# The same instructions in another order: 860 words of a hand-ordered list for attention and an MLP

## The chip, the cores and the metric

The kernel runs on one core of a Trainium2 chip. The metric is the device time of one execution in microseconds; runs are compared by the median of several. The engines are TensorE (PE, with its weight loads as PEld), VectorE (DVE), ScalarE (ACT), GpSimd (POOL) and SyncE (SP), which only issues DMAs. Each engine works through its own instructions strictly in the order in which the program gives them, and waits for other engines by semaphores.

## The reference

Attention with a causal mask and a bias from a running sum, over 8 batches of 8 heads, 576 rows and 64 columns, then a layer norm and a two-layer MLP (512 to 2048 to 512) with a residual:

```python
scores = scale * np.matmul(q, k.transpose(0, 1, 3, 2))
cum = np.cumsum(np.maximum(s, 0.0), axis=-1)
bias = -(cum[:, :, :, None] - cum[:, :, None, :])
scores = np.where(causal, -1000000000.0, scores + np.minimum(bias, 0.0))
attn = np.exp(scores - np.max(scores, axis=-1, keepdims=True))
attn = attn / (np.sum(attn, axis=-1, keepdims=True) + 1e-09)
x = np.matmul(attn, v)            # heads side by side: (8, 576, 512)
xn = (x - mu) / np.sqrt(var + 1e-06) * g_ln
out = x + np.maximum(xn @ w_ch1, 0.0) @ w_ch2
```

## The kernel before

Rows are taken in tiles of 128 (four, and a tail of 64 rows, tile 4). The work of a batch is: load k, q and v; transpose k and q; scores in PSUM banks; exp on ScalarE into the SBUF tile `er`; a mask on the diagonal blocks on GpSimd; the product with v; a division by the row sums on VectorE; the layer norm's statistics and the normalised rows `xn`; a transpose of those by DMA; the first product with w1 and relu (into `hT`); the second product with w2; scale, residual and store.

All of it is one straight program. A fixed opening issues the first loads, mostly on GpSimd's queue, which also converts them. After it the order is a list of 1238 words, `PLAN` (L1278), written out by hand: a word such as `vm.2.0:P` names a step, its arguments and, behind a colon, the engine (A ScalarE, D VectorE, P GpSimd). A loop calls the steps one after another, and each step issues its few instructions on its engines. The list thus sets the order on each engine, and only that: two words that are neighbours in the list but on different engines have no order between them beyond what data and buffers ask.

The words that matter here:

- The running sums of the bias, in three pieces of bf16: `relu`, `relur` and `scan.0/1/2` (the scan over columns 0 to 127, 128 to 255, 256 to 575), `hi`, `sub`, `mid`, `lo` split a piece, `tc` transposes the pieces on PE and `bc` copies them into the rows of k and q (L281, L285). `m` is two memsets (L1219).
- Batch 0, tile by tile: `cq`, `ck` convert the first tile of q and k (L140); `T.t.g` transposes tile t of head group g on PE (L948, into a bank `trt`), `e.t.g` copies it out to `kq`; `S.t.g.i` is a bank of scores, `x` its exp (L987); `V` the product with v (L1028), `N` its division, `L.t` the normalised rows, `X.t` their transposes on PE, `y.t` the copy out; `M` and `r` are a first product in pieces and its relu.
- Batch 1, head by head: `Q.k.n`/`Q.q.n` transposes a pair of heads (L322, `trqk`), `E...0` and `E...1` copy its halves out; `aug` and `a3` bring the bias rows by DMA on SP (L264, L266); `s` scores and exp, `d` the tail, `v` product, `n` division, `l` the normalised rows, `D` their transpose by DMA on SP (L732).
- Batches 2 to 7, by pairs of heads: `lr.b.t` loads tile t of k and q on SP, `cr.b.t.u` converts it on GpSimd (L217), `tr` transposes by DMA on SP (L224); `lv.b.t` loads v on SP (L205), `vm.b.t` weighs it on GpSimd (L232). Batch 2 has its k and q from GpSimd's own loads (`lp`) with `O2`, `F` and `G` (copy, transposes, copy out; L360). `B2.n` is a burst of six banks of scores for pair n (L548), `bx.n.x` one exp of the six (L553), `bm.n.x` one mask (L492), `sd`, `se`, `sm` the same for the tail keys; `Y.n.i` is the product with v for head i of the pair (L627), `K.n.i` its division; `ga` and `la` make statistics and normalised rows, `Da` their transpose by DMA.
- `u` and `U` each run one unit of the MLP from a queue: four matmuls of 512 columns, of the first product with a relu behind it (on ScalarE for `u`, on VectorE for `U`; L761, L750, L752) or of the second (L780), after whose last quarter VectorE makes the result (L792) and SP stores it (L813).
- `w2.n` loads a quarter of w2 on GpSimd's queue. `to` closes the first set of PSUM banks (2 for `trt`, `ph` and `py`, 3 for scores, 2 for transposes and products, 1 more) and opens the second (2 for products and `py`, 6 for bursts and `ph`).

Buffers are slots: 8 for loaded rows of 128 x 512 f32, 6 more for v from `to` on, `er` for four heads. A step that needs a slot waits until the last user of an earlier tenant is done, wherever in the list that user stands on its own engine.

Of the kernel before, what the change touches and what calls it, by code (L numbers as in the profile page):

```python
# [16 lines left out]
P = 128  # L17
# [13 lines left out]
def fast_path(  # L31
# [13 lines left out]
    B, H, S, D = q.shape  # L45
# [13 lines left out]
    G = 4  # L59
# [881 lines left out]
    E = {"A": "act", "D": "dve", "P": "pool"}  # L941
# [241 lines left out]
    def raise_flag(count, ones, n):  # L1183
# [95 lines left out]
        relur.1 lr.3.0 relu.0 scan.0 scan.1 cq hi.0 qu.1 hi.1 sub.0 mid.0 lo.0 relur.2 sub.1 scan.2 W.2  # L1279
        tc.0 bc.0 ck.0 T.0.1 T.0.0 mid.1 lo.1 tc.1 e.0.1:D bc.1 T.1.1 hi.2 sub.2 e.0.0:A S.0.0.0 T.1.0  # L1280
        W.1 m mid.2 lo.2 La.3 tc.2 e.1.1:D x.0.0.0 V.0.0 bc.2 e.1.0:A S.0.1.0 N.0.0 x.0.1.0 S.1.1.0
        x.1.1.0 T.2.1 bc.4 e.2.1:D S.1.1.1 x.1.1.1 T.2.0 S.1.0.1 x.1.0.1 e.2.0:D V.0.1 S.1.0.0 N.0.1
        S.2.1.2 x.2.1.2 T.3.0 x.1.0.0 e.3.0:D qu.2 S.2.0.2 S.2.1.0 x.2.0.2 aug L.0 x.2.1.0 T.3.1 S.3.0.1
        x.3.0.1 V.1.0 e.3.1:D qu.3 La.2 N.1.0 V.1.1 N.1.1 L.1 S.2.0.0 x.2.0.0 S.2.0.1 x.2.0.1 S.3.0.2
        x.3.0.2 X.0 y.0:A S.3.1.2 S.2.1.1 x.2.1.1 V.2.0 N.2.0 x.3.1.2 X.1 y.1:D S.3.0.0 x.3.0.0 V.2.1
        M.0.1.0 B.0.1 M.0.1.3 S.3.0.3 x.3.0.3 M.0.1.2 N.2.1 L.2 M.0.1.1 r.0.1:A M.0.0.0 M.0.0.2 Q.q.4
        B.1.1 O E.q.4.0:A M.0.0.3 E.q.4.1:A V.3.0 N.3.0 S.3.1.1 x.3.1.1 M.0.0.1 r.0.0:D S.3.1.3 S.3.1.0
        T.4.0 e.4.0:D X.2 y.2:D x.3.1.3 Q.k.4 E.k.4.0:D T.4.1 e.4.1:D x.3.1.0 S.4.0.1 x.4.0.1 S.4.0.0
        M.0.2.0 M.0.2.2 x.4.0.0 M.0.2.3 V.3.1 E.k.4.1:D N.3.1 B.2.1 S.4.1.1 x.4.1.1 u d.8 L.3 M.0.2.1
        Q.q.5 r.0.2:D B.1.0 s.8 u X.3 S.4.1.0 x.4.1.0 y.3:D Sk xk E.q.5.1:D E.q.5.0:A B.0.0 B.3.0 a3 u  # L1290
        v.8 qu.4 qu.5 Q.k.5 lp.9 E.k.5.0:D u E.k.5.1:D V.4.0 N.4.0 s.9 cr.3.0.1 n.8 V.4.1 N.4.1 Q.q.6
        E.q.6.0:A u B.2.0 d.10 s.10 wr Q.k.6 E.k.6.0:D A.0 v.9 lp.10 w2.2 lr.3.1 E.k.6.1:D n.9 u U
        E.q.6.1:A s.11 Q.k.7 Q.q.7 E.q.7.0:A lp.11 La.6 E.k.7.0:D E.q.7.1:A U U E.k.7.1:D v.10 n.10
        cr.3.0.0 U d.12 s.12 U v.11 n.11 ga.1.0.0 A.2 d.14 s.13 O2.k.9:A u w2.3 B.3.1 v.12 n.12 ga.1.0.3
        s.14 O2.k.8:A A.1 me wT lv.2.0 wx vo.2:P U v.13 n.13 ga.1.1.2 s.15 cr.3.1.1 U O2.q.9:A ga.1.0.2
        F.k.8 v.14 ga.1.0.1 F.k.9 G.k.9:A n.14 U u A.3 R vm.2.0:P lr.3.2 v.15 cr.3.2.0 O2.k.11:A lv.2.1
        lv.2.2 vm.2.1:P G.k.8:A ga.1.1.1 u lv.2.3 u O2.q.8:A ga.1.1.3 F.q.9 G.q.9:A n.15 ga.1.2.1
        O2.q.11:A lv.2.4 lr.3.3 cr.3.2.1 cr.3.1.0 ga.1.2.0 ga.1.1.0 ga.1.2.3 ga.1.2.2 l.0 O2.k.10:A u u
# [4 lines left out]
        K.8.0 bx.9.5 K.8.1 bm.9.3 bx.9.2 bm.9.0 bx.9.3 bx.9.1 bm.9.1 u bm.9.2 U u u Y.9.0 vm.3.0:P  # L1303
        ga.1.2.4 la.1.4 B2.10 bx.10.0 K.9.0 bx.10.3 bx.10.4 bx.10.2 bx.10.5 cr.3.4.0 bm.10.3 bx.10.1
        Y.9.1 U K.9.1 u u tr.3.2.4 U u tr.3.4.5 bm.10.1 Y.10.1 lv.3.1 bm.10.0 B2.11 bx.11.0 bx.11.4
        lv.3.2 bx.11.5 lv.3.3 K.10.1 bm.10.2 Y.10.0 K.10.0 bm.11.2 ga.2.0.0 lv.3.4 bx.11.2 bm.11.0 La.4
        bx.11.1 u ga.2.1.2 ga.2.0.3 U u tk.3 cr.4.1.1 lr.4.2 bx.11.3 Y.11.0 K.11.0 bm.11.3 u sd.3 U
        bm.11.1 u se.3 ga.2.0.1 lr.4.3 cr.4.0.1 vm.3.1:P Y.11.1 K.11.1 lv.4.0 lv.4.1 vm.3.4:P lr.4.4 u
# [273 lines left out]
```

## Time and profile before

| | |
|---|---|
| runs shown | 348.24 us median of 3 (347.27 to 348.98) |
| the profiled execution | 347.05 us around a span of 345.5 us |
| mean granted TensorE clock | 0.992 |
| instructions | 8016, of them 3067 matmuls |
| HBM | 37.11 MB read, 9.44 MB written |

The profile is of one execution. A span is the time from the first to the last instruction. In its lines, `out<-in` are the program's tiles, xN counts instructions, and what stands in brackets or behind an arrow is the idle time of the engine just ahead of an instruction and what ended it. Views used below: the page (shares of the engines, and 40 slices of the span in tenths), windows (busy time of each engine in stretches), waits (who waited for whom), groups of instructions by line and shape, the timeline of an engine (start, length, what), and the chain of waits that ended last.

### The profile page before, as it was taken

Reading aid. Unit: us, or ns where it says so; the run is one execution under the profiler, and the core shown is the slowest. Engines: PE = TensorE matmul, PEld = TensorE weight load, DVE = VectorE, ACT = ScalarE, POOL = GpSimd, SP = SyncE. Lnnn points to the kernel's source line nnn. Section 1 sums busy time; section 2 is a strip of 40 time slices with the busy share of each in tenths; the row PEclk is TensorE's granted clock in tenths of the full one; section 3 lists DMA queues with packets and bytes.
Section 4 is the critical chain, followed back from the end, with each engine's and each line's share of the span. In section 5 each row is a group of like instructions: output and inputs, shape, how many; then the busy total and the mean of one; then the engine's idle time right before and its main releaser. Section 6 shows DMA issues by size and latency. Waiting matters only on the chain.

```text
span 345.5 us, 8016 instructions
## 1 busy us (share of the span) xinstructions
PE 332.2 (96%) x3067; PEld 185.6 (54%) x3093; DVE 206.6 (60%) x593; ACT 185.4 (54%) x343; POOL 168.8 (49%) x306
## 2 busy tenths in 40 slices
PE   5999999989999999999999999999999999999994
PEld 2998856545545555555555555554545444444443
DVE  6687798826675687556653774557448614523412
ACT  4698889677655686357636863486434204202200
POOL 8897677696577775865685377441301001000000
PEclk9899999999999999999999999999999999999998
DMA  9999999899989999998686965600420141011022
GB/s 147 185 191 174 201 194 204 191 221 237 202 197 241 224 223 196 225 216 183 154 190 176 227 112 138 139 2 2 113 71 0 23 132 46 2 76 47 0 64 65
DMA packets 147963, 48.59 MB, mean 141 GB/s; under 512 B 135281, under 2 KB 143761, under 8 KB 147921
## 3 DMA queue, kind: packets, MB, share of 16 engines
q1 hardware_dynamic: 121856, 38.34, 51.2%
q0 software_dynamic: 24304, 8.92, 21.6%
q10 hardware_dynamic: 1760, 0.79, 0.9%
q8 instruction: 25, 0.41, 0.5%
q14 instruction: 18, 0.14, 0.1%
HBM read 37.11 MB, written 9.44 MB: 135 GB/s over the span
## 4 chain that ended last, share of the span: by engine, by line
PE 82%; SPq 6%; DMA 4%; POOL 3%; DVE 2%; issue 1%; ACT 0%
PE ph L761 32%; PE py L780 32%; PE pot L627 7%; SPq L205 5%; DMA rowtmp<-in_v_dram 3%; PE sa L548 2%; PE trt L948 2%; PE sc L548 1%; PE sb L548 1%; DMA c_in<-in_s_dram 1%; POOL v_bf L232 1%; PE ph L1072 1%; PE st L970 1%; POOL kq L217 1%; PE pot L1028 1%
## 5 line engine op out<-in xcount | busy, mean ns | idle before, releaser
L780 PE MATMUL py<-w_bf,hT 128*128 128x512 bf16 (+2 forms) x583 | 128.4, 367 | 1.8 <-issue 0.3
L761 PE MATMUL ph<-xT,w_bf 128*128 128x512 bf16 x480 | 109.8, 379 | 0.0
L752 ACT ACTIVATE hT<-ph 128x512 bf16<-128x512 f32 x97 | 58.0, 602 | 82.0 <-PE ph L761 80.6
L780 PEld LDWEIGHTS <-hT 128*128 128x128 bf16 x608 | 56.1, 98 | 60.9 <-issue 0.7
L761 PEld LDWEIGHTS <-w_bf 128*128 128x128 bf16 x544 | 51.0, 98 | 56.3
L492 POOL TENSOR_SCALAR_AFFINE_SELECT er<-er 128x256 bf16<-128x256 bf16 x96 | 38.5, 415 | 61.8 <-ACT er L553 46.9
L792 DVE SCALAR_TENSOR_TENSOR yo<-py,rstd,xb 128x512 f32<-128x512 f32 x32 | 24.0, 751 | 48.5 <-PE py L780 44.2
L750 DVE TENSOR_SCALAR hT<-ph 128x512 bf16<-128x512 f32 x39 | 26.8, 690 | 27.0 <-PE ph L761 26.2
L553 ACT ACTIVATE er<-sb 128x512 bf16<-128x512 f32 x48 | 28.2, 609 | 21.1 <-PE sb L548 21.1
L553 ACT ACTIVATE er<-sa 128x512 bf16<-128x512 f32 x48 | 28.6, 608 | 13.3 <-PE sa L548 10.5
L232 POOL TENSOR_TENSOR v_bf<-rowtmp,wt 128x512 bf16<-128x512 f32 (+1 forms) x30 | 32.4, 1085 | 1.9 <-DMA rowtmp<-in_v_dram 1.8
L627 PEld LDWEIGHTS <-er 128*128 128x128 bf16 x672 | 25.7, 97 | 10.8 <-POOL er L492 1.5
L553 ACT ACTIVATE er<-sc 128x512 bf16<-128x512 f32 x48 | 28.8, 613 | 4.1 <-PE sc L548 4.1
L627 PE MATMUL pot<-v_bf,er 128*128 128x66 bf16 x672 | 28.1, 193 | 1.1 <-POOL er L492 1.0
L684 POOL TENSOR_TENSOR rstd<-rstd,mhalf 128x4 f32<-128x4 f32 (+1 forms) x8 | 8.8, 1097 | 38.8 <-DVE rstd L683 35.7
L644 DVE TENSOR_REDUCE sums<-pot 128x5 f32<-128x10 f32 x48 | 8.0, 166 | 31.2 <-PE pot L627 30.9
L710 DVE SCALAR_TENSOR_TENSOR xn<-xb,mv,gb 128x512 bf16<-128x512 f32 x28 | 25.2, 898 | 1.0
L217 POOL CAST kq<-rowtmp 128x512 bf16<-128x512 f32 (+1 forms) x30 | 20.7, 699 | 8.9 <-DMA rowtmp<-in_k_dram 8.8
L669 DVE BATCH_NORM_STATS2 stats<-xb 128x6 f32<-128x128 f32 (+1 forms) x84 | 23.8, 323 | 0.4
L647 DVE TENSOR_TENSOR xb<-pot,rinvs 128x256 f32<-128x256 f32 x48 | 20.4, 425 | 1.6
L548 PEld LDWEIGHTS <-kq 64*128 64x128 bf16 x360 | 11.2, 94 | 10.1 <-issue 4.7
L987 ACT ACTIVATE er<-st 128x512 bf16<-128x512 f32 x24 | 13.1, 604 | 3.6 <-PE st L978 2.3
(172 smaller groups left out, 394.9 us busy)
## 6 DMA issues: line engine op xcount, KB each, us to landing
out_dram<-yo SPq DMA_DIRECT2D x32, 256.0 KB
rowtmp<-in_v_dram SPq DMA_DIRECT2D x24, 256.0 KB
rowtmp<-in_k_dram SPq DMA_DIRECT2D x20, 256.0 KB
rowtmp<-in_q_dram SPq DMA_DIRECT2D x20, 256.0 KB
w_bf<-in_moe_w_ch_dram POOLq DMA_DIRECT2D x8, 512.0 KB, 9.3
kp<-in_k_dram POOLq DMA_DIRECT2D x8, 144.0 KB, 9.4
qp<-in_q_dram POOLq DMA_DIRECT2D x8, 144.0 KB, 9.8
v_bf<-in_v_dram POOLq DMA_DIRECT2D x8, 128.0 KB, 7.7
```

Source lines behind the costliest of these rows:

```text
L217: nc.gpsimd.tensor_copy(out=rows[b % 2][0:pn, t, u], in_=loaded.pop(("kq"[u], b, t))[0:pn])
L232: e.tensor_tensor(out=v_bf[b % 2][0:pn, t, :, 0:D], in0=loaded.pop(("v", b, t))[0:pn], in1=wt[0:pn, t, b, :].unsqueeze(2).to_broadcast([pn ...
L492: nc.gpsimd.affine_select(out=out, in_=out, compare_op=ALU.is_ge, fill=0.0, base=0, pattern=pattern, channel_multiplier=-1,)
L548: nc.tensor.matmul(a, lhsT=lhsT, rhs=rhs, start=True, stop=True)
L553: nc.scalar.activation(out=er[:, 2 * n % 4 + i, o : o + 512], in_=bank["B", n].pop((name, i)), func=ACT.Exp, scale=scale,)
L627: nc.tensor.matmul(pot[:, t, :], lhsT=cols, rhs=v_bf[b % 2][:, kb, h, :], start=(kb == 0), stop=(kb == t),)
L710: nc.vector.scalar_tensor_tensor(out=xn, in0=tiles[t], scalar=mvs[b][:, t, 0:1] if b > 0 else mean0[:, t : t + 1], in1=gb, op0=ALU.subtrac ...
L750: nc.vector.tensor_scalar_max(out=dst, in0=ph, scalar1=0.0)
L752: nc.scalar.activation(out=dst, in_=ph, func=ACT.Relu)
L761: nc.tensor.matmul(ph, lhsT=w1_bf[:, kd, fb * P : (fb + 1) * P], rhs=xT[:, :, kd, :], start=(kd == 0), stop=(kd == KD - 1),)
L780: nc.tensor.matmul(py[t], lhsT=hT[:, fb, t * P : (t + 1) * P], rhs=w2_bf[:, fb, c0:c1], start=(fb == 0), stop=(fb == FB - 1),)
L792: nc.vector.scalar_tensor_tensor(out=yo, in0=py[t], scalar=rs, in1=x[:, c0:c1], op0=ALU.mult, op1=ALU.add)
```

## The change

The list's first 860 words stand in another order; each word occurs as often as before, and the remaining 378 are the same. Seventeen copies and evictions change engines: to VectorE go `e.1.0`, `y.0`, `r.0.1`, `E.q.4.1`, `E.q.5.0`, `E.q.6.0`, `E.q.7.0`, `E.q.7.1`, `G.k.8` and `G.k.11`; to ScalarE `e.2.1`, `e.4.0`, `E.k.4.0`, `r.0.2`, `E.k.5.0`, `E.k.6.1` and `E.k.7.0`. There are 112 `u` and 19 `U` among the 860 words before and after, at other places. In the diff, cut to the stretches that the text speaks of, the lines of the list are as they stand:

```diff
     PLAN = """
-        relur.1 lr.3.0 relu.0 scan.0 scan.1 cq hi.0 qu.1 hi.1 sub.0 mid.0 lo.0 relur.2 sub.1 scan.2 W.2
-        tc.0 bc.0 ck.0 T.0.1 T.0.0 mid.1 lo.1 tc.1 e.0.1:D bc.1 T.1.1 hi.2 sub.2 e.0.0:A S.0.0.0 T.1.0
...
-        T.4.0 e.4.0:D X.2 y.2:D x.3.1.3 Q.k.4 E.k.4.0:D T.4.1 e.4.1:D x.3.1.0 S.4.0.1 x.4.0.1 S.4.0.0
...
-        lr.3.4 vm.2.3:P vm.2.2:P cr.3.3.0 u F.q.8 G.q.8:A F.q.11 G.q.11:A u u O2.q.10:A F.k.10 G.k.10:A
-        F.k.11 G.k.11:A tk.2 qu.6 qu.7 l.1 l.2 l.3 u D F.q.10 G.q.10:A cr.3.3.1 vm.2.4:P to u lv.3.0
-        B2.8 bx.8.3 bx.8.0 vo.3:P bx.8.2 ga.1.0.4 u lr.4.0 lr.4.1 u ga.1.1.4 bx.8.4 bm.8.2 sd.2 se.2
-        sm.2 bx.8.5 bx.8.1 bm.8.0 bm.8.3 bm.8.1 cr.3.4.1 u tr.3.0.2 u B2.9 Y.8.0 bx.9.0 bx.9.4 Y.8.1
...
+        m relu.0 relur.1 scan.0 scan.1 hi.0 hi.1 W.2 sub.0 sub.1 mid.1 cq mid.0 W.1 lo.1 ck.0 lo.0 tc.0 bc.0
+        tc.1 T.0.1 e.0.1:D T.0.0 relur.2 bc.1 S.0.1.0 T.1.1 T.1.0 scan.2 e.0.0:A e.1.1:D hi.2 x.0.1.0 O S.0.0.0
...
+        x.1.0.0 T.3.1 L.0 N.1.1 e.2.1:A S.2.0.0 V.1.0 N.1.0 S.3.0.2 x.2.0.2 x.2.0.0 X.0 L.1 S.2.1.1 x.2.0.1
+        x.2.1.1 S.2.1.2 V.2.0 S.3.0.0 X.1 S.3.0.3 x.2.1.2 y.0:D x.3.0.0 S.2.1.0 x.2.1.0 e.3.1:D M.0.0.0 M.0.0.2
...
+        E.q.4.0:A x.3.1.3 M.0.1.3 S.3.1.2 M.0.0.3 S.3.1.0 L.2 x.3.1.2 X.2 Q.k.4 S.3.1.1 T.4.0 x.3.0.1 r.0.1:D
+        e.4.0:A La.3 qu.3 r.0.0:D x.3.1.0 T.4.1 V.3.0 y.2:D qu.4 M.0.2.0 x.3.1.1 S.4.0.1 E.k.4.0:A u x.4.0.1
...
+        E.q.6.1:A u a3 E.k.6.0:D V.4.1 E.q.6.0:D n.9 qu.5 lv.2.2 s.10 u N.4.1 d.10 U s.11 Q.k.7 O2.k.8:A v.10
...
+        O2.q.10:A l.3 ga.1.0.1 cr.3.3.0 F.q.10 u O2.q.11:A u O2.k.11:A l.1 l.2 D U F.q.11 F.k.11 lv.2.0 u lv.2.1
+        G.k.11:D G.k.10:A tk.2 lr.3.2 lr.3.4 u to G.q.10:A vm.2.4:P lv.3.2 B2.8 cr.3.0.0 G.q.11:A cr.3.1.0
+        bx.8.0 u ga.1.2.4 bx.8.5 bx.8.3 sd.2 bm.8.3 U bx.8.4 u vo.2:P bx.8.1 bx.8.2 B2.9 u bm.8.2 bm.8.0 se.2
+        bx.9.4 bx.9.1 bx.9.0 qu.6 vm.2.0:P bm.8.1 u u bx.9.2 u vm.2.1:P bx.9.5 sm.2 cr.3.2.0 U bm.9.3 cr.3.4.0
+        bx.9.3 u cr.3.2.1 lv.3.0 Y.8.0 B2.10 bm.9.0 cr.3.4.1 bm.9.2 K.8.0 tr.3.0.2 bx.10.0 tr.3.4.5 Y.8.1
...
```

More of the change, by code (lines that the diff above doesn't have):

```diff
@@ L1289, in fast_path @@
[L1289 to L1298, printed above, removed]
@@ L1304, in fast_path @@
[L1304 to L1308, printed above, removed]
@@ L1359, in fast_path @@
-        u u u vl u u u u u u u u u u u u u u u u u u
+        m relu.0 relur.1 scan.0 scan.1 hi.0 hi.1 W.2 sub.0 sub.1 mid.1 cq mid.0 W.1 lo.1 ck.0 lo.0 tc.0 bc.0
+        tc.1 T.0.1 e.0.1:D T.0.0 relur.2 bc.1 S.0.1.0 T.1.1 T.1.0 scan.2 e.0.0:A e.1.1:D hi.2 x.0.1.0 O S.0.0.0
+        sub.2 mid.2 lo.2 V.0.1 x.0.0.0 e.1.0:D S.1.1.0 x.1.1.0 tc.2 bc.2 qu.1 V.0.0 bc.4 aug S.1.0.1 T.2.0
+        x.1.0.1 S.1.1.1 La.4 T.3.0 S.1.0.0 N.0.1 x.1.1.1 e.2.0:D T.2.1 N.0.0 V.1.1 S.2.0.2 e.3.0:D qu.2 S.2.0.1
+        x.1.0.0 T.3.1 L.0 N.1.1 e.2.1:A S.2.0.0 V.1.0 N.1.0 S.3.0.2 x.2.0.2 x.2.0.0 X.0 L.1 S.2.1.1 x.2.0.1
@@ new lines, in fast_path @@
+        bm.30.3 bx.31.1 bm.31.1 Y.30.1 K.30.1 ga.7.1.0 ga.7.0.4 bm.31.3 ga.7.1.4 ga.7.1.3 bx.31.4 bm.31.2 u U
+        Y.31.1 U bm.31.0 ga.7.1.2 u Y.31.0 K.31.0 K.31.1 ga.7.2.2 ga.7.2.3 ga.7.2.0 u u ga.7.1.1 ga.7.2.4 u u u
+        U ga.7.0.0 u u u u ga.7.2.1 la.7.0 la.7.1 la.7.2 la.7.3 Da.7.0 u u u u u u u u u u u u u u u u u U u U u
+        la.7.4 U u U u u u u U U gd u Da.7.4 u u u u u u u u u u u u u u u u U u u u U U U u u U u U U U U fl u
+        u u u u u vl u u u u u u u u u u u u u u u u u u
```

114 lines of the change are left out of this document (56 added, 58 removed).

## The prediction

> **What bounds the kernel now.** I read the page first, for the shares of the engines.
>
> ```profile
> span 345.5 us, 8016 instructions
> ...
> PE 332.2 (96%) x3067; PEld 185.6 (54%) x3093; DVE 206.6 (60%) x593; ACT 185.4 (54%) x343; POOL 168.8 (49%) x306
> ...
> PEclk9899999999999999999999999999999999999998
> DMA  9999999899989999998686965600420141011022
> ```
>
> PE is busy for 332.2 of 345.5 us, so only the 13.3 us without a matmul, and whatever runs at a lower clock, can be won by an order. DMA is full for the first third. The windows say where the idle time lies (first number the length, second PE busy; then weight loads, DVE, ACT, POOL, the clock, the DMA share and GB/s).
>
> ```profile
> 5.40:8.80 3.40, 1.30 (x11) 0.64 (x10) 2.57 (x10) 1.93 (x5) 3.33 (x7) 1.00 1.64 184
> 8.80:12.20 3.40, 3.11 (x33) 2.90 (x30) 2.24 (x7) 1.38 (x2) 2.72 (x4) 0.50 2.14 163
> ...
> 15.60:32.00 16.40, 15.41 (x322) 14.91 (x320) 14.12 (x43) 13.69 (x26) 14.74 (x25) 1.00 1.62 186
> 32.00:56.00 24.00, 23.53 (x344) 16.91 (x341) 20.19 (x49) 20.75 (x41) 17.08 (x33) 1.00 1.33 194
> 56.00:70.00 14.00, 13.58 (x126) 7.67 (x127) 10.82 (x31) 11.10 (x19) 10.51 (x18) 1.00 1.00 202
> 70.00:77.00 7.00, 5.94 (x60) 2.96 (x59) 2.03 (x4) 5.49 (x11) 6.71 (x16) 1.00 1.00 223
> 77.00:175.00 98.00, 97.39 (x945) 52.23 (x951) 65.55 (x197) 61.14 (x117) 66.80 (x124) 1.00 0.98 206
> ```
>
> Length less PE busy is 0.99, 0.47, 0.42 and 1.06 us in the four stretches from 15.6 to 77, and 0.61 in the 98 us behind them. From 77 us on there is next to nothing to win; the changed words reach to about 247 us, so there the new order can only hold what is. The last view names the waits of PE.
>
> ```profile
> PE trt L948 <- DVE rowb L285: 1.6, 1, 1.6
> PE idle L858 <- DVE warm L875: 1.5, 1, 1.5
> PE pot L627 <- POOL er L492: 1.0, 1, 1.0
> PE trqk L322 <- DVE xT L142: 0.6, 1, 0.6
> PE after L1369 <- DVE mark L1367: 0.5, 1, 0.5
> ...
> PE trt L948 <- DVE rowb L281: 0.3, 1, 0.3
> PE trx L743 <- DVE xn L710: 0.3, 1, 0.3
> PE py L780 <- DMA w_bf<-in_moe_w_ch_dram: 0.3, 1, 0.3
> ```
>
> The rows shown add up to 6.1 us. The first memset (1.5) and the end mark (0.5) stay; with three small rows left out, some 5 us are the most that a better order can take away, apart from the half-clock stretch.
>
> **The change, part by part.** No instruction is added or removed and none changes shape, so PE's own work stays. Each term below is a wait that moves.
>
> *The start.* These rows show what T.0.1 (the first L948) is late for.
>
> ```profile
> 3.48 0.34 DVE L925 CAST identf<-ident 64x64 f32<-64x64 bf16 x1
> 4.20 0.28 DVE L1196 SCALAR_TENSOR_TENSOR hT<-hT 64x128 f32<-64x128 f32 x1 [0.38 <-DMA hT<-in_s_dram]
> ...
> 6.58 0.28 DVE L311 TENSOR_TENSOR hT<-c_sc,c 64x128 f32<-64x128 f32 x1
> ...
> 7.29 0.60 ACT L140 CAST rowb<-tiletmp 128x512 bf16<-128x512 f32 x1
> 7.42 0.88 DVE L292 TENSOR_TENSOR_SCAN c_sc<-c_one,c_sc,c_in 64x320 f32<-64x320 f32 x1 [0.57 <-ACT c_in L1222]
> 8.53 1.64 PE L948 MATMUL trt<-ident,rowb 128*68 128x128 bf16 x16 [1.61 <-DVE rowb L285]
> ...
> 11.27 0.51 DVE L1219 MEMSET rowb<- 32x544 uint32 x1 [0.17 <-issue]
> ```
>
> bc.0 stands behind scan.2, which waits for a load. The new list puts scan.2 behind bc.1. Against it, m goes first: its 0.51 us memset starts at 3.82 and ends at 4.33, so relu.0 slips by about 0.2 us. The short DVE operations ended at 6.86; with that slip and lo.1 (of the same kind, 0.28, now ahead of lo.0) they end at 7.34. The transposes tc.0 and bc.0 add some 0.5, and ck.0, now behind mid.1 and cq on ScalarE, ends near 8.1. T.0.1 then starts near 8.15, not 8.53. Behind it S.0.1.0 needs only e.0.1, where both halves were made first, and e.1.0 and y.0 leave ScalarE. I take -0.6; the bounds are +0.5 (ck.0 or m late) and -1.9 (both trt waits gone).
>
> *The engines.* Seventeen copies change places: ten go to VectorE, seven to ScalarE.
>
> ```profile
> L140 ACT COPY kq<-trt 68x1024 bf16<-68x1024 bf16 x2 | 2.0, 1002 | 1.4 <-PE trt L948 1.4
> L142 DVE COPY kq<-trt 68x1024 bf16<-68x1024 bf16 x6 | 4.1, 684 | 1.6 <-PE trt L948 1.5
> ```
>
> A full e costs 1.00 us on ScalarE against 0.68 on VectorE. The two G on VectorE have no row there; I bound them by these two and take 0.8 between them, as for a copy at large. Three copies net, some 2.4 us, go from ScalarE to VectorE, over 40 us in which both have 2 us of slack or more in each stretch (windows above). Alone it is worth nothing; it counts where a transpose waits for its bank.
>
> *15.6 to 32 us.* Q.k.4 stood right behind X.2 and y.2 and waited 0.6 for y.2 to empty a bank (trqk, DVE xT). Now it stands ahead of y.2 and takes a bank that N.2.1 or the two halves of E.q.4, one on each engine, empty. X.1's wait for L.1 (0.3) may stay; L.1 has three score groups and V.2.0 ahead of X.1, as before. VectorE is the tighter engine here (14.12 of 16.40). I take -0.8; bounds -1.0 and +1.0, should X.1 or X.3 wait for VectorE.
>
> *32 to 70 us.* w2.3 goes up by some 15 us of matmul work, so the wait for w_bf (0.3) falls. Of the other idle time (0.47 and 0.42 in the two windows) I take a third. POOL's opening section no longer shares the first DMA time with lr.3.0, so what waits for its last memsets comes earlier. I take -0.5; bounds -0.9 and +0.5.
>
> *70 to 77 us.* Here the masks of the first burst, bm.8, stood behind v rows and casts on POOL:
>
> ```profile
> 55.25 10.12 SPq L205 DMA_DIRECT2D rowtmp<-in_v_dram x4
> ...
> 70.65 4.08 SPq L732 DMA_TRANSPOSE xT<-xn  x1
> ...
> 75.73 0.39 SPq L205 DMA_DIRECT2D rowtmp<-in_v_dram  x1
> ```
>
> ```profile
> 70.01 0.39 PE L548 MATMUL sa<-kq 64*128 64x512 bf16 x2
> ```
>
> ```profile
> 65.50 1.04 POOL L232 TENSOR_TENSOR v_bf<-rowtmp,wt 128x512 bf16<-128x512 f32 x1 [1.20 <-DMA rowtmp<-in_v_dram]
> ...
> 76.05 1.12 POOL L492 TENSOR_SCALAR_AFFINE_SELECT er<-er 128x256 bf16<-128x256 bf16 x3
> ...
> 79.13 1.04 POOL L232 TENSOR_TENSOR v_bf<-rowtmp,wt 128x512 bf16<-128x512 f32 x1
> ```
>
> ```profile
> 77.85 3.45 PE ph L761 x16
> 81.30 0.45 PE pot L627 x15
> 81.75 0.32 PE sa L548 x2
> ...
> 82.51 0.56 PE pot L627 x15
> ```
>
> Now bm.8 goes ahead of vm.2.0 and vm.2.1, but lv.2.0 and lv.2.1 go from far ahead of D to behind it in SP's queue. What stands between D and Y.8.0 on PE grows from five units to twelve: 12 x 0.86 (3.45 for four units) plus two bursts of 0.76 (81.75 to 82.51) and some 0.7 of transposes and tails is 12.6 us of cover. The chain beside it: D was issued 0.64 after the burst (70.01) that stands one unit behind it, so it runs some 1.5 late; 4.08 for D; two issues, 1.0; landing; then two v rows (2.08) and three masks (1.12) on POOL, 3.2. The landing has two bounds: under 3.4 (issued 75.73, used without a wait at 79.13) and 10.2 (55.25 to 65.5). DMA is less loaded behind D than at 55, so I take the lower one: 1.5 + 4.08 + 1.0 + 3.4 + 3.2 = 13.2 against 12.6, a wait of 0.6 where PE's idle time in the window was 1.06. Less what waited in PE's queue unseen, the term is -0.7; bounds -1.3 and +6.3.
>
> *Behind 77 us.* The new list has three pairs of bursts only two units apart (B2.12, 14, 18 and their successors), where the old one kept three or more. A burst, two units and two Y are 0.76 + 1.72 + 0.90 = 3.4 us, in which ScalarE must empty six banks.
>
> ```profile
> L553 ACT ACTIVATE er<-sb 128x512 bf16<-128x512 f32 x48 | 28.2, 609 | 21.1 <-PE sb L548 21.1
> ```
>
> Six of 0.609 end to end would be 3.65, 0.25 too long; the units there are of the second product, which ask nothing of ScalarE. I take +0.2; bounds 0 and +0.8.
>
> Sum: -0.6 - 0.8 - 0.5 - 0.7 + 0.2 = -2.4. The profiled execution took 347.05 us around its span of 345.5, so it would become 344.65; the runs shown have a median of 348.24, and on that scale the forecast is 345.8.
>
> **The rivals.** *A: all waits go.* The window 8.8 to 12.2 runs at clock 0.50, behind one in which PE was busy for 1.30 of 3.40. If the earlier transposes keep the clock up, the 3.11 us there shrink by up to half, of which I count 1; and some 2 us of the 5 that are not yet in the sum, 342.8. Against it: the new start leaves PE idle between the warm-up and tc.0 too. [...]
>
> *B: nothing moves.* The waits are replaced by others of the same length, since VectorE and ScalarE have the same work in the first 32 us: 348.2. For it speaks that ScalarE and VectorE are at 83 and 86% there.
>
> *C: slower, the v rows late.* One mechanism: lv.2.0 and lv.2.1 behind D. From a landing of about 5.5 us on it costs more than the rest brings. With 8 us, between the bounds, Y.8.0 waits 5.2, 4.1 more than now, and the other terms give 1.7: 350.6; with 10.2, 352.9. PE cannot pass Y.8.0, so every matmul behind it waits. For it: the DMA share is 1.00 from 56 to 77, and more loads stand ahead of these two than before. [...] Against C: less is queued once D is reached.
>
> That the change does something else than it says is no rival: every word occurs as often as before.
>
> **How the numbers follow.** Forecast 345.8 (its own range 344.0 to 347.0): 0.42. A 342.8: 0.13. B 348.2: 0.09. C 350.6: 0.36. A measurement of this kernel tells 0.5% (1.74 us) from no change, so faster means under 346.5 and slower over 350.0. Of the forecast 0.35 lies under 346.5; with A faster is 0.48. C gives 0.33 of slower and B's edge 0.02; the rest, 0.17, is the same. The range reaches from A's better edge, 342.5, to C's upper part, 352.0.
>
> **What would show it.** T.0.1 at 8.0 to 8.3; no wait of trqk for xT; no wait for w_bf; a wait of pot under 0.7 at Y.8.0, with vm.2.1 just ahead of it; PE idle under 1 us from there to 175. C is shown by a wait of pot for the v rows and D's issue just ahead of them. I am wrong if PE waits anywhere behind the first burst for more than 2 us, for example for the six banks of B2.13, or at s.12, whose extra rows (a3) are now loaded later.

## The result, and the profile after

The changed kernel takes 348.98 us in the median of 20 runs (347.81 to 351.48), the kernel before 347.52 us in 20 runs beside them (345.91 to 349.08). The ratio is 1.0056, with a 95% interval of 1.0034 to 1.0077: about half a per cent slower, where 0.7% faster was forecast. Ratios, here and below, are formed from all runs; they are not the quotient of the two medians and can differ from it by some tenths of a per cent (the quotient is 1.0042 here). The profiled execution is one of the longest of the 20, 351.27 us around a span of 349.8, so its waits show more than the median lost. A second profile of the same kernel (experiment 1) is of a run of 347.60 us; both are read below.

The page of the kernel after, its first lines:

```profile
span 349.8 us, 8004 instructions
...
PE 333.8 (95%) x3067; PEld 186.4 (53%) x3093; DVE 204.3 (58%) x588; ACT 187.1 (53%) x348; POOL 168.6 (48%) x306
...
PEclk9998999999999999999999999999999999999999
DMA  9999999679999999999929967500330051011022
```

PE's busy time grew by 1.6 us, its idle time by 2.7. The first is a stretch at a lower clock, the 8 in the fourth slice: in the second profile, which has no such stretch, PE is busy for 331.9 us, where it was 332.2 before. The dent in the clock was in the second slice before. The windows of before, read again on the kernel after (length, PE busy, weight loads, DVE, ACT, POOL, clock, DMA share, GB/s):

```profile
5.40:8.80 3.40, 2.64 (x22) 1.37 (x21) 2.06 (x10) 2.01 (x5) 3.32 (x7) 1.00 2.36 158
8.80:12.20 3.40, 3.02 (x51) 2.59 (x48) 2.71 (x6) 2.39 (x5) 3.40 (x5) 1.00 2.19 148
...
15.60:32.00 16.40, 14.68 (x264) 13.95 (x262) 11.56 (x34) 11.27 (x20) 15.65 (x26) 0.90 1.68 183
32.00:56.00 24.00, 23.43 (x361) 17.50 (x359) 17.32 (x43) 21.97 (x44) 10.43 (x21) 1.00 1.19 202
56.00:70.00 14.00, 13.16 (x139) 7.88 (x140) 12.51 (x38) 11.52 (x22) 10.71 (x21) 1.00 0.75 151
70.00:77.00 7.00, 6.32 (x52) 2.72 (x50) 3.22 (x7) 4.04 (x8) 4.12 (x10) 1.00 0.66 151
```

From 8.8 to 12.2 PE does 51 matmuls at full clock, where it did 33 at half clock; how much of this the order brought is taken up below the table. Between 15.6 and 32 it does 264, where it did 322: there the lead is lost, and VectorE and ScalarE, both near 14 of 16.4 us before, stand idle for 5 us each. They are not too busy, they are held up. The waits of PE say where (engine, line, whom it waited for; total, times, longest):

```profile
PE st L970 <- ACT er L987: 1.6, 1, 1.6
PE idle L858 <- DVE warm L875: 1.5, 1, 1.5
PE pot L627 <- POOL v_bf L232: 1.2, 1, 1.2
...
PE pot L583 <- DVE xm L604: 0.7, 1, 0.7
...
PE sa L548 <- DVE kq L142: 0.6, 1, 0.6
PE sa L548 <- DMA kq<-kq: 0.5, 1, 0.5
```

Gone are the rows of before for the first transposes (trt, 1.6), for Q.k.4 (trqk, 0.6), for w_bf (0.3) and for the masks at Y.8.0 (1.0). The largest new one, 1.6, is a score product of batch 0 that waits for an exp. The timeline of the kernel after, of all engines, follows it back (start, length, engine, what, and the idle time just ahead with what ended it):

```profile
21.15 1.57 ACT L987 ACTIVATE er<-st 128x512 bf16<-128x512 f32 x3 [0.53 <-PE st L970]
...
21.40 0.42 PE L322 MATMUL trqk<-ident,qp 96*128 96x96 bf16 x6
...
23.23 0.56 POOL L924 MEMSET kq<- 128x512 bf16 x1
...
23.83 0.80 DVE L142 COPY kq<-trqk 64x576 bf16<-64x576 bf16 x1 [2.43 <-POOL kq L924]
...
24.66 0.79 ACT L140 COPY kq<-trqk 64x576 bf16<-64x576 bf16 x1 [1.94 <-DVE kq L142]
...
25.32 1.55 ACT L987 ACTIVATE er<-st 128x512 bf16<-128x512 f32 x3
...
25.96 0.38 PE L970 MATMUL st<-kq 68*128 68x128 bf16 x4 [1.59 <-ACT er L987]
```

Read from the bottom: PE waits for an exp, which stands on ScalarE behind `E.q.4.0`, which begins 0.03 us after VectorE's half `E.q.4.1` has ended, ahead of which VectorE has stood idle for 2.43 us, the last part of them for a memset on POOL. (The transposes of `Q.q.4` that it copies end at 21.82, so some 2.0 of the 2.43 us are the memset's.) That memset (L924) clears the pad columns of `kq[2]`, the tile that both halves write. In the source the halves write other columns of that tile than the memset does, and still the copy began only 0.04 us behind the memset's end; whether the wait goes by the whole tile, no run tried apart. The memset is no word of the list; it stands late in the fixed opening, in POOL's queue behind other memsets and the DMA issues of the first loads. The same instructions in the timelines of the kernel before, POOL's, PE's and ScalarE's:

```profile
24.48 0.56 POOL L924 MEMSET kq<- 128x512 bf16 x1
```

```profile
24.55 0.42 PE L322 MATMUL trqk<-ident,qp 96*128 96x96 bf16 x6
```

```profile
25.08 1.61 ACT L140 COPY kq<-trqk 64x576 bf16<-64x576 bf16 x2
```

There PE's transposes ended at 24.97, the memset at 25.04, and the copies began at 25.08, both on ScalarE, which had been free since 24.94. From the end of the memset to the copy it is 0.04 us, as much as in the kernel after (23.79 to 23.83), where the memset did release it. So the copies had no room, or only some hundredths of a us, and no wait showed it. Under the new order POOL's opening is 1.25 us earlier (23.23 for 24.48), but `Q.q.4` comes 3.15 us earlier (21.40 for 24.55), and its copies now stand in front of exps and divisions that PE needs sooner.

To see what each stretch of the list brought, take the time at which PE begins a certain word and subtract the work of PE that the list puts ahead of it (0.864 for a unit of the MLP, 4 x 0.216, as 20 of its matmuls take 4.32 us from 77.81 to 82.13 in the kernel after; 0.75 for a burst, there 76.18 to 76.94; in the kernel before 0.45 for a T, 14.54 to 14.99, and 0.886 for an s, 31.89 to 32.78; and so on, the same for all columns, so that only differences between columns are read; the sums are good to some 0.1 us, but each column is one execution). The starts are those of the trace:

```
start of             before   after  again  memset up | work ahead: old list, new list
first V (L1028)       13.59   11.46  11.47     11.46  |   3.53     3.61
s.8 (first L390)      31.89   32.33  31.36     29.45  |  19.91    18.89
B2.8 (first L548)     70.01   72.49  71.52     69.61  |  55.90    55.90
Y.8.0 (first L627)    76.51   82.13  81.16     79.25  |  61.09    65.41
the last matmul      340.80  344.80 341.71    340.95  | 327.96   327.96

change of PE's lateness against the kernel before, by stretch
                    forecast   after  again  memset up
to the first V          -0.6    -2.2   -2.2      -2.2
to s.8                  -0.8    +3.7   +2.7      +0.8
to B2.8                 -0.5    +1.0   +1.0      +1.0
to Y.8.0                -0.7    -1.2   -1.2      -1.2
to the end              +0.2    +2.7   +0.6      +1.7
sum                     -2.4    +4.0   +0.9      +0.1
```

"Again" and "memset up" are the second profile of the changed kernel and the kernel of experiment 2. Two terms came out with the sign of the forecast and larger, two had the wrong sign, and the last one differs from run to run.

The column "before" is one execution too. Runs 4 and 12 have the same list as the kernel before up to B2.8, and in their profiles the first V begins at 11.90 and 13.52, `s.8` at 30.44 and 31.82 and B2.8 at 69.19 and 68.76. Measured against these two, the first row of the changed kernel is -0.5 or -2.1, the second +3.4 or +3.7 (+2.5 or +2.7 in the second profile), and the third +0.4 or +2.2. The signs of these rows stand; the sizes of the first and the third do not.

Most of the first row is PE's clock. Between 8.8 and 12.2 us the clock of the old start was 0.50 in the profiles of before and of run 11, 0.52 in run 12 and 0.66 in run 6, but 1.00 in run 4. That of the new start was 1.00 in seven profiles and 0.65 and 0.56 in those of runs 3 and 7. So the half-clock stretch comes and goes with either order; the new one had it less often. Where both starts had the full clock (run 4, 11.90, against 11.46) the order is worth 0.5 us.

### The profile page after: what moved, and what is told of

It reads as the page before. It is cut to its first block, busy times and chain, and to the rows that moved or that the text cites. A ratio compares the mean times of both kernels' runs of the same rounds, so it can differ in the third digit from the quotient of the medians.

```text
span 349.8 us, 8004 instructions
## 1 busy us (share of the span) xinstructions
PE 333.8 (95%) x3067; PEld 186.4 (53%) x3093; DVE 204.3 (58%) x588; ACT 187.1 (53%) x348; POOL 168.6 (48%) x306
## 4 chain that ended last, share of the span: by engine, by line
PE 71%; POOL 10%; DVE 7%; DMA 5%; issue 3%; ACT 2%; POOLq 0%; SPq 0%; ACTq 0%
PE py L780 31%; PE ph L761 25%; PE pot L627 5%; PE sa L548 2%; DMA kq<-kq 2%; POOL rowb L179 2%; PE ph L1072 2%; DMA kq<-rowb 2%; DMA rowtmp<-in_v_dram 2%; DVE xn L710 1%; PE sc L548 1%; PE sb L548 1%; POOL v_bf L191 1%; POOL v_bf L232 1%; DVE kq L142 1%
## 5 line engine op out<-in xcount | busy, mean ns | idle before, releaser
L752 ACT ACTIVATE hT<-ph 128x512 bf16<-128x512 f32 x105 | 62.7, 605 | 85.6 <-PE ph L761 84.4
L492 POOL TENSOR_SCALAR_AFFINE_SELECT er<-er 128x256 bf16<-128x256 bf16 x96 | 39.5, 429 | 48.6 <-ACT er L553 33.3
L553 ACT ACTIVATE er<-sb 128x512 bf16<-128x512 f32 x48 | 28.9, 609 | 20.8 <-PE sb L548 19.9
L750 DVE TENSOR_SCALAR hT<-ph 128x512 bf16<-128x512 f32 x31 | 21.4, 691 | 31.6 <-PE ph L761 30.0
L710 DVE SCALAR_TENSOR_TENSOR xn<-xb,mv,gb 128x512 bf16<-128x512 f32 x28 | 24.5, 875 | 1.0
L217 POOL CAST kq<-rowtmp 128x512 bf16<-128x512 f32 (+1 forms) x30 | 18.2, 621 | 13.2 <-DMA rowtmp<-in_k_dram 10.7
```

The lines of the kernel that those rows point to most:

```text
L492: nc.gpsimd.affine_select(out=out, in_=out, compare_op=ALU.is_ge, fill=0.0, base=0, pattern=pattern, channel_multiplier=-1,)
L553: nc.scalar.activation(out=er[:, 2 * n % 4 + i, o : o + 512], in_=bank["B", n].pop((name, i)), func=ACT.Exp, scale=scale,)
L710: nc.vector.scalar_tensor_tensor(out=xn, in0=tiles[t], scalar=mvs[b][:, t, 0:1] if b > 0 else mean0[:, t : t + 1], in1=gb, op0=ALU.subtrac ...
L750: nc.vector.tensor_scalar_max(out=dst, in0=ph, scalar1=0.0)
L752: nc.scalar.activation(out=dst, in_=ph, func=ACT.Relu)
```

## The experiments

Theory M: a wait that stands in the order itself, above all for the pad memset, eats the lead. Its rivals: that the loads further on set the time whatever PE does (L), that the loss is chance (V), that it lies elsewhere in the list (R against F), or in the engines (H against O).

**1. The changed kernel again.** No edit.

> The changed kernel once more, for a second profile. In the first one PE lost 1.75 us at 24.15 (a score product that waits for ScalarE, which waits for VectorE's E.q.4.1, which waits 2.43 us for POOL's memset of the pads of kq[2]) and the clock fell to 0.50 behind it; further on 0.79 at 71.5 (the banks of B2.8), 0.7 at 97 (k rows by DMA) and 1.33 at 170 (v rows). Theory M (a fixed order is the cause): the waits at 24 and 71 are there again within 0.3 us, since they hang on the order of the queues alone. Theory V (chance): the waits for loads at 97 and 170 differ by more than 0.5 us between the two profiles, and the time of the run goes with them. Time 348.5 to 349.5 by both.

Measured: 348.35 us in the median (347.58 to 351.35), ratio 1.0049 (1.0025 to 1.0073); the profiled run took 347.60. The waits at 24 (now 1.05, with 0.37 for the load of q just ahead of `Q.q.4`) and at 71.5 (0.6) are there again; those for loads at 97 and 170 are not among its waits at all. The median is just under the expected range. As expected, the order's own waits stay and the loads' waits come and go; with what else differs behind Y.8.0 they make 2.1 (2.7 less 0.6 in the table) of the 3.7 us between the two profiled runs. The wait at 24 shrank by more than the expectation allowed, 0.54 us, but it ends at 25.96 in both profiles: `Q.q.4` began 0.53 later in the second, and the memset had the last word in both. One more difference is the clock. Windows of the first profile, then of the second:

```profile
24.00:26.00 2.00, 0.41 (x8) 0.29 (x6) 1.86 (x6) 1.34 (x3) 2.00 (x3) 1.00 1.27 193
...
28.00:29.50 1.50, 1.50 (x27) 1.50 (x26) 1.11 (x4) 1.50 (x4) 1.43 (x3) 0.50 2.28 156
```

```profile
24.00:26.00 2.00, 0.95 (x18) 0.83 (x16) 1.86 (x6) 1.33 (x3) 2.00 (x3) 1.00 1.26 196
...
28.00:29.50 1.50, 1.50 (x42) 1.50 (x40) 1.27 (x5) 1.50 (x4) 1.20 (x2) 1.00 2.24 162
```

With 1.59 us idle between 24 and 26 the clock falls to 0.50 two microseconds later, with 1.05 it does not. The 1.0 by which the two profiles differ at `s.8` lies behind 25.96, so it is this stretch, less a wait of 0.45 of the second profile. The two figures are no threshold: in run 6 a wait of 1.06 us at the start was followed by a clock of 0.50 to 0.66, and in run 7 the clock was 0.56 there though, behind the first memset's 1.5, no single wait up to there was over 0.51.

**2. The pad memset earlier.**

```diff
+    nc.gpsimd.memset(kq[2][:, :, :, S:SP], 0.0)
     ld_cast_tile("k", NF)
     ld_cast_tile("q", NF)
...
     ld_cast_pair(5)
     ld_w1(2)
-    nc.gpsimd.memset(kq[2][:, :, :, S:SP], 0.0)
```

> One memset of POOL's opening section, the pads of kq[2] that E.q.4 waits for, goes up by seven DMA issues and seven memsets (some 7 us). Theory M: the wait of PE at 24 us (1.75) goes, the half-clock stretch that follows it (clock 0.50 from about 28 to 31) goes too or falls on idle time, 2.0 to 2.7 us in all: 346.2 to 347.0. Rival L (later limits): PE comes earlier to loads and casts that have a pace of their own, so the time won at 24 is waited for again by 77 us, and the time stays at 348.3 to 349.3.

Measured: 347.42 us (345.59 to 349.57), ratio 1.0015 (0.9992 to 1.0038), 0.93 less than the changed kernel on the same chip; it cannot be told from the kernel before. The profiled run took 347.00. Its waits:

```profile
PE idle L858 <- DVE warm L875: 1.5, 1, 1.5
PE pot L627 <- POOL v_bf L232: 1.1, 1, 1.1
...
PE pot L583 <- DVE xm L604: 0.7, 1, 0.7
...
PE sa L548 <- DVE kq L142: 0.6, 1, 0.6
```

The wait for the exp at 24 us is gone and so is the half-clock stretch: `s.8` starts 1.9 us earlier than in the second profile of the changed kernel (29.45 for 31.36). Theory M holds for the mechanism. At the end 0.8 of these 1.9 is left; 1.1 went for a v row near 166 us, as rival L said. The result lies between the two ranges.

**3 and 4. Half of the new list, cut at the first burst.** The list is made of one order up to the word `B2.8` (319 words of the new one, 327 of the old; the expectations count one less), and of the words that remain in the other order. The lines below are shorthand for the two lists, not lines of the kernels.

```diff
-    PLAN = NEW
+    PLAN = NEW[:NEW.index("B2.8")] + [w for w in OLD if w not in the first part]   # 3
+    PLAN = OLD[:OLD.index("B2.8")] + [w for w in NEW if w not in the first part]   # 4
```

> The new order up to the word B2.8 (318 words), behind it the old order of the words that remain. From the two profiles, the lateness of PE against its own matmuls differs by +0.4 us at 72 us (1.6 won at the start, 2.0 lost behind it) and by +3.8 at the end. Theory R (the loss lies behind the first burst): 347.4 to 348.0, within 0.4 us of the kernel before. Rival F (the loss lies in front of it): 348.7 or more, the whole of the change.

> The counterpart: the old order up to the word B2.8 (326 words), behind it the new order of the words that remain. Theory R (the loss lies behind the first burst): 348.7 to 349.5. Rival F (it lies in front): 347.2 to 347.8, as the kernel before.

Measured: the third takes 355.56 us (ratio 1.0257, 1.0224 to 1.0290), the fourth 347.06 (1.0009, 0.9987 to 1.0031). The third has a wait of its own, made by the seam:

```profile
PE pot L627 <- POOL er L492: 6.3, 1, 6.3
```

At the seam v rows and casts that the old order had done by then stand on POOL ahead of the masks of the first burst, and PE waits 6.3 us at Y.8.0. So this run does not decide (355.56 less 6.3 is 349.3, with whatever the seam costs besides). The fourth speaks for rival F: with the old order in front, the new one behind the first burst costs nothing that can be told from noise (its median is even under that of the kernel before, 347.20 beside it). The loss belongs to the part in front, even where it shows up later. Two reservations: joining the lists also gives five evictions of the MLP another engine, and the fourth profile had the full clock at the start.

**5 and 6. The engines alone.**

```diff
-    e.1.0:D e.2.1:A y.0:D E.q.4.1:D r.0.1:D e.4.0:A E.k.4.0:A E.q.5.0:D ... E.q.7.1:D     # new order, tagged words only
+    e.1.0:A e.2.1:D y.0:A E.q.4.1:A r.0.1:A e.4.0:D E.k.4.0:D E.q.5.0:A ... E.q.7.1:A     # 5: 15 of 17 as before
...
-    e.1.0:A e.2.1:D y.0:A r.0.1:A E.q.4.1:A ... G.k.8:A G.k.11:A                          # old order, tagged words only
+    e.1.0:D e.2.1:A y.0:D r.0.1:D E.q.4.1:D ... G.k.8:D G.k.11:D                          # 6: all 17 as in the change
```

> The changed order, but 15 of the 17 copies that changed engines are back on their old engine (the two G on VectorE stay, since the order needs them there). Theory O (the order costs, not the engines): PE still waits 1.2 to 1.8 us near 24 to 26, for the pad memset that E.q.4 waits for, and the time is that of the changed kernel, 348.0 to 348.8. Rival H (the engines cost): where the two halves of one bank are copied by two engines, the second begins when the first ends (E.q.4: VectorE's half ends at 24.63, ScalarE's begins at 24.66), so a pair on one engine costs no handover and blocks one engine only: 347.0 to 347.5.

> The old order with the 17 new engines. The prediction's term for them is nothing: 346.8 to 347.6. Rival H (halves of one bank on two engines run one behind the other, and hold both): half of the loss or more is here too, 347.9 to 348.6.

Measured: 354.41 us for the new order with the old engines (ratio 1.0213, 1.0183 to 1.0244), 348.86 for the old order with the new engines (1.0045, 1.0027 to 1.0064). The fifth is out of both ranges, O's too: rival H is wrong as put, since the old engines make the new order much worse. Its profile shows PE waiting 1.6 us for a ScalarE copy at 61 us and 1.5 and 1.0 us for q and k rows by DMA, and B2.8 begins at 77.45, where the changed kernel has it at 72.49. The sixth says that the engines are not free in the old order either. One place where its time goes is seen in its waits, and on VectorE's timeline:

```profile
PE py L780 <- DVE yo L792: 1.8, 1, 1.8
```

```profile
68.44 0.76 DVE L142 COPY kq<-trp 128x576 bf16<-128x576 bf16 x1 [2.00 <-PE trp L360]
69.11 0.23 DVE L687 BATCH_NORM_AGGREGATE mv<-stats 128x2 f32<-128x18 f32 x1
69.37 0.90 DVE L710 SCALAR_TENSOR_TENSOR xn<-xb,mv,gb 128x512 bf16<-128x512 f32 x1
...
72.14 0.74 DVE L792 SCALAR_TENSOR_TENSOR yo<-py,rstd,xb 128x512 f32<-128x512 f32 x1
```

`G.k.11`, now on VectorE, is 0.76 us for which VectorE first waits 2.00 us for PE's transposes. Three rows of `xn` queue up behind it, and the result `yo` behind those is late too: PE waits 1.8 us for it. In the same profile the wait for the masks at Y.8.0, 1.0 before, is gone, so 0.8 is left of the 1.8. The profiled run, 347.45, is one of the fastest of its kernel; the median lies above even the range that H gave, and the rest of it stays open. The engine of an eviction is here not a matter of 0.4 us more or less but of what stands behind it in the queue.

**7 and 8. The new start alone, with and without the memset moved.** The first 95 words in the new order (up to `Q.q.4`), the rest in the old.

```diff
-    PLAN = NEW
+    PLAN = NEW[:NEW.index("Q.q.4")] + [w for w in OLD if w not in the first part]   # 7; 8 with the memset as in 2
```

> The first 95 words in the new order (up to the word Q.q.4), behind them the old order of the rest, nothing else. At 16 us PE is then 1.6 us ahead of the kernel before. Theory P (POOL's opening section has a pace of its own, and the v rows behind it too): the lead is used up by the wait of E.q.4 for the pad memset (0.3 to 1.2) and by a longer wait of Y.8.0 for POOL's masks (1.2 us now, up to 2.5): 346.8 to 347.5. Rival G (the lead stays): 345.4 to 346.0.

> The same with the pad memset of kq[2] moved up as in the run before with that memset. Theory P: the lead of 1.6 us is still there at 40 us, but the wait of Y.8.0 for POOL's masks grows from 1.2 to 2.5 us or more, and the time is 346.6 to 347.3. Rival G: nothing later takes the lead back: 345.2 to 345.9, and this is the best of the kernels so far.

Measured: 348.29 us (1.0048, 1.0027 to 1.0068) and 348.68 (1.0045, 1.0020 to 1.0070), both slower than the kernel before, where at most no change was expected. That the lead does not stay is confirmed (rival G is out); that it is lost at Y.8.0 is not. In the profile of the seventh the lead is only 1.1 us at the first V (12.52, with a clock of 0.56 ahead of it); it is used up by 32 us (two waits for exps, 0.9 in all), and the wait at Y.8.0 is 1.0 as before. In that of the eighth 0.9 us of it is still there at `s.8`, and by B2.8 PE is 2.7 us later than before. One part of that are the v rows:

```profile
PE pot L583 <- DMA v_bf<-in_v_dram: 1.7, 4, 0.6
```

The v rows of batch 1, which POOL's opening issues in its turn, have not landed when PE reaches the first product that needs them. Another is a clock of 0.50 from 38 to 41 us. In both runs the median lies above what these waits explain, and that part stays open.

**9 and 10. Two later waits mended, then a third.** Both with the memset up.

```diff
-    O2.k.9:A wr B.3.0 u n.12
+    O2.k.9:A B.3.0 u n.12 wr
...
-    l.1 l.2 D U F.q.11 F.k.11 lv.2.0 u lv.2.1 G.k.11:D
+    l.1 U F.q.11 F.k.11 G.k.11:D l.2 D lv.2.0 u lv.2.1
...
# 10 besides: lv.5.1 ahead of lv.6.2, and
-    cr.6.2.1 u u U ga.4.1.0 ... vm.6.2:P u ga.4.0.3 vm.5.4:P u Y.20.0
+    vm.5.4:P cr.6.2.1 u u U ga.4.1.0 ... vm.6.2:P u ga.4.0.3 u Y.20.0
```

> The new order with the pad memset up, and two words moved that PE still waited for between 40 and 72 us: wr (1.23 us of VectorE) behind n.12, which a PV pass waits for (0.82), and G.k.11 with F.k.11 ahead of l.2 and D, so that the banks of B2.8 are free 0.8 us earlier. Both theories expect B2.8 some 1.5 us earlier than in the run with the pad memset alone (B2.8 started there at 69.6). Theory L (loads further on have a pace of their own): the lead is waited for again by 170 us, at the k rows by DMA near 94 and the v rows near 166, and the time is 346.8 to 347.6, as with the memset alone. Rival G (the lead stays): 345.4 to 346.2.

> The same, and the load lv.5.1 nine units of PE earlier (ahead of lv.6.2) and the weighing vm.5.4 ahead of the cast of cr.6.2.1, so that the last v row of Y.20 (1.22 us of wait near 166 with the pad memset alone) is there in time. Theory L: now the lead reaches the end, less what the k rows near 94 take (0.4): 345.2 to 346.2. Rival G' (the loads push each other back, another one is late): 346.8 to 347.6.

Measured: 347.40 us (1.0016, 0.9988 to 1.0044) and 348.47 (1.0055, 1.0026 to 1.0084). In the tenth's profile B2.8 is 0.9 us earlier than with the memset alone, but 0.7 comes back as a wait of PE for `yo`, and 0.8 for VectorE's `mv` and 0.6 for k rows by DMA wait further on. The ninth came out as theory L has it, without the gain of G'. The tenth lies above both ranges: where waits were taken away others appeared (0.7, 0.8 and 0.6), but its profiled run, 347.34, is its fastest, so these waits do not explain its median, and that stays open. The ninth's profile is one of its longest runs (350.20), and shows what varies:

```profile
PE trqk L322 <- DMA qp<-in_q_dram: 1.7, 1, 1.7
```

This is `Q.q.4` again, waiting for its q rows: 1.7 us in this profile, 0.4 in the second one of the changed kernel, none in the first, on programs that are the same up to there but for the place of one memset. In the new order `Q.q.4` stands close to where its load lands.

**11. The old order with the memset late.**

```diff
     ld_w1(2)
-    nc.gpsimd.memset(kq[2][:, :, :, S:SP], 0.0)
...
     for t in range(NT):
         ld_cast_v(1, t)
+    nc.gpsimd.memset(kq[2][:, :, :, S:SP], 0.0)
```

> The kernel before, with the pad memset of kq[2] moved behind the five v loads that follow it in POOL's opening section: it ends near 29.2 instead of 25.04, where the old order's E.q.4 began at 25.08. Theory M (this memset was the hidden bound of the old order too, met with 0.04 us to spare): PE waits 2 to 4 us near 26 to 29, and the time is 348.8 to 351. Rival C (there is cover behind it): less than 0.7 us, 346.7 to 347.7.

Measured: 349.72 us, ratio 1.0080 (1.0053 to 1.0107), 3.3 more than the kernel before in the same runs: theory M. ScalarE's timeline, and the windows of the same kernel:

```profile
30.29 1.60 ACT L140 COPY kq<-trqk 64x576 bf16<-64x576 bf16 x2 [3.95 <-POOL kq L927]
```

```profile
30.00:32.60 2.60, 0.13 (x5) 0.04 (x2) 1.89 (x3) 2.28 (x4) 1.45 (x3) 0.81 2.25 161
32.60:36.00 3.40, 3.40 (x52) 3.39 (x52) 0.17 (x1) 1.87 (x4) 2.18 (x3) 0.50 1.68 173
36.00:38.00 2.00, 2.00 (x26) 2.00 (x24) 1.65 (x6) 0.64 (x2) 1.58 (x3) 0.50 1.23 191
```

A memset of half a microsecond on the engine that nobody suspects holds ScalarE for 3.95 us (the transposes that it copies had ended at 26.37) and PE for 2.5, and in this profile a clock of 0.50 for more than 5 us follows. The profiled run, 350.97, is the longest of this kernel; the median is what the verdict goes by.

**12. The one piece that the change did improve, put into the old order.** At Y.8.0 the old order has POOL run four small instructions for batch 3 (`vo.3`) ahead of the masks that PE waits for.

```diff
-    bx.8.3 bx.8.0 vo.3:P bx.8.2 ga.1.0.4 u ... bm.8.0 bm.8.3 bm.8.1 cr.3.4.1
+    bx.8.3 bx.8.0 bx.8.2 ga.1.0.4 u ... bm.8.0 bm.8.3 bm.8.1 vo.3:P cr.3.4.1
```

> The kernel before with a single word moved: vo.3 (1.05 us of POOL, four small weighings for a batch that is needed much later) goes behind the masks of the first burst (bm.8), for which Y.8.0 waited 0.98 us at 75.5. Theory K (the one wait that the change truly removed is worth its length, where the loads behind it are not asked for earlier than they land): PE runs through at Y.8.0, 0.7 to 1.0 us less, 345.4 to 345.9 beside 346.4 for the kernel before in the last runs. Rival L (a wait further on takes it back, as with the leads of the other runs): within 0.3 us of the kernel before.

Measured: 346.28 us (344.45 to 349.48) beside 347.07 (345.66 to 348.27), ratio 0.9986 (0.9959 to 1.0012). The median is lower by 0.8, and the lowest runs, 344.45 to 344.51, are below all others of this study, but the interval includes 1: not shown to be faster. It lies between the two ranges expected. The profiled run, 344.45, is the fastest of all. In it B2.8, which stands ahead of the word that was moved, already begins 1.25 us earlier than in the kernel before (68.76 for 70.01), so of the 2.3 us at Y.8.0 (74.21 for 76.51) only 1.05 can be the change. Its waits, all rows down to 0.4:

```profile
PE idle L858 <- DVE warm L875: 1.5, 1, 1.5
PE trt L948 <- DVE rowb L285: 1.4, 1, 1.4
PE trqk L322 <- DVE xT L142: 0.6, 1, 0.6
PE after L1363 <- DVE mark L1361: 0.5, 1, 0.5
PE trc L275 <- DVE c L308: 0.4, 1, 0.4
```

The wait for the masks is gone, and in this profile no other has come in its place. Its ratio is the lowest of the kernels run.

## Why the prediction was wrong, point by point

- *The start, -0.6.* The first T began at 8.14, where about 8.15 was forecast; with the old start it began between 8.01 and 8.86 in five profiles. At equal clock the order brought 0.5 by the first V (run 4), so the term was right in mechanism and size. The further 1.7 in the table is the clock, which stayed at 1.00 here as rival A had it. It was no part of the forecast, and in one profile of the old start it came without the change, so it is in part luck, though seven of nine profiles of the new start had it.
- *The engines, 0.* Wrong, and the count was too. The list's units also change engines at 26 places, and the groups of relu evictions, before and after, are these:

```profile
L750 DVE TENSOR_SCALAR hT<-ph 128x512 bf16<-128x512 f32 x39 | 26.8, 690 | 27.0 <-PE ph L761 26.2 <-ACT er L553 0.2
```

```profile
L750 DVE TENSOR_SCALAR hT<-ph 128x512 bf16<-128x512 f32 x31 | 21.4, 691 | 31.6 <-PE ph L761 30.0 <-ACT hT L752 1.0
```

Eight of 0.69 us left VectorE for ScalarE, against the 2.4 us that the copies moved the other way. More than the size it is the method that failed: slack in a window did not show what a queue holds up, as runs 5 and 6 show with opposite signs.
- *15.6 to 32, -0.8: the step that failed.* "Now it stands ahead of y.2 and takes a bank that N.2.1 or the two halves of E.q.4, one on each engine, empty." `Q.k.4` did not wait any more, as forecast. But its bounds, -1.0 and +1.0, were drawn round VectorE's load, and the thing that ended the wait was POOL: I asked what each copy reads, not what it writes to. Measured: +2.7 to +3.7, of which 1.9 is the memset by run 2, and another 1.0 the half clock of the one profile that had it. With the memset moved up the stretch still loses 0.8, where 0.8 was to be won; what that is made of was not shown. And the two halves are not emptied side by side. VectorE's waits in the kernel after have a row that is not among those of before:

```profile
DVE kq L142 <- ACT kq L140: 2.5, 4, 0.9
```

Four times VectorE's copy begins when ScalarE's of the same kind ends, so in those four cases a pair on two engines took the time of both (0.80 and 0.79 us, one behind the other, for `E.q.4`). In the source the halves go to interleaved columns of one tile; whether that, or something else, ties them was not tried.
- *32 to 70, -0.5.* The wait for w_bf went and POOL's memsets came 1.25 us earlier, as forecast. But `wr` (1.23 us) on VectorE ahead of a division cost 0.7, and `G.k.11` behind two rows of `xn` kept the banks of B2.8 for another 0.6: +1.0 in the table, +0.4 and +2.2 against runs 4 and 12. Both were in the list and were not priced.
- *70 to 77, -0.7.* -1.2. The masks are no longer late, and neither are the v rows. On the timeline of the kernel after (SP's issue of both rows, their weighing on POOL, and Y.8.0):

```profile
73.78 1.81 SPq L205 DMA_DIRECT2D rowtmp<-in_v_dram  x2
...
77.79 1.04 POOL L232 TENSOR_TENSOR v_bf<-rowtmp,wt 128x512 bf16<-128x512 f32 x1
...
79.16 1.04 POOL L232 TENSOR_TENSOR v_bf<-rowtmp,wt 128x512 bf16<-128x512 f32 x1
...
82.13 0.59 PE L627 MATMUL pot<-v_bf,er 128*128 128x66 bf16 x14
```

Both are weighed without a wait, so the first had landed within 4.0 us of 73.78, near the lower bound taken, and the second within 5.4; D took 1.89 and not 4.08. Rival C did not come about here: the DMA share, 1.00 from 56 to 77 in the kernel before, was 0.75 from 56 to 70 and 0.66 from 70 to 77. The 6.3 of run 3 are another case, masks that stand behind v rows and casts in POOL's queue.
- *Behind 77, +0.2.* +0.6 and +2.7 in two profiles of one program, +1.7 with the memset up: not the burst pairs, as far as the waits show, but loads that land later than PE arrives: POOL waits 5.0 us for a v row in the first profile and 1.7 in the second. Of the three pairs that the prediction has two units apart, B2.18 has three between.
- *The clock.* In the kernel before the clock was 0.50 from 8.8 to 12.2, behind 3.4 us in which PE was busy for 1.30; the longest single wait of PE was 1.6 us in both kernels. In the first profile of the changed kernel a half clock fell on denser work (0.50 from 28 to 31, PE busy for all 3.0 us), and `s.8` began 1.0 us later than in the second, which had 1.00 there. The two differ in the idle time between 24 and 26 (1.59 and 1.05 us), and with that wait gone (run 2) there was no half clock either. But runs 6 and 7 had a clock of 0.66 and 0.56 at the start behind single waits of 1.06 and of at most 0.51, so what sets off a half clock, and when it falls, was not shown.
- *The rivals.* B, that waits are replaced by others of the same length, was nearest (348.2 against 348.98), with too small a chance (0.09). It named VectorE and ScalarE; the replacement stood on POOL.
- *The signs.* Of the five that were named, four came out: the first T, no wait of `trqk` for `xT`, none for w_bf and none at Y.8.0. PE's idle time from Y.8.0 to 175 was 2.9 us (1.4 in the second profile) and not under 1. None of the five looked at `E.q.4`, where the lead was lost.

## What to carry to other kernels

When an order moves work earlier, list everything that the moved step needs, above all one-time work outside the order (memsets, opening loads), with its end time in the trace; a step that today starts 0.04 us after such an event may have no room, though its profile shows no wait. Here a lead in front of the loads that POOL's opening issues was worth nothing (348.29 and 348.68 us in runs 7 and 8, beside 347.04 for the kernel before; in run 8 PE waited 1.7 us for v rows of that opening). Price an eviction by who queues behind it while it waits, not by its duration (run 6: a copy of 0.76 us, behind which three rows of `xn` and the result `yo` stood, and PE waited 1.8 us). Before rearranging what PE does not wait for, try the last wait that it really has: run 12 did, with the lowest ratio here, though not shown to be under 1.

## What the runs showed that was not expected

In run 11 a half-clock stretch covers all of 32.6 to 38 us, though PE is busy in all of it; in the changed kernel's first profile it lasted some 3.4 (0.93 from 27 to 28, 0.50 up to 31, 0.86 from 31 to 32). At the start the stretch comes and goes from profile to profile, with the old order (1.00 in run 4, 0.50 in the kernel before) and with the new (0.56 in run 7, 1.00 in the changed kernel). And a load that PE meets about when it lands costs one run nothing and another 1.7 us (`Q.q.4`). Whether that is why the changed kernel's times are as they are was not tried: its upper ten runs lie above every run of the kernel before that was timed beside them, but the two sets of 20 span nearly the same, 3.7 and 3.2 us.
